# Three of four row tiles of the later quarters are transposed by DMA instead of TensorE, x is loaded a quarter ahead, one pool holds the PSUM banks, and VectorE adds into banks that are still accumulating

## The chip, the cores and the metric

The kernel runs on one core of one Trainium2 chip. The metric is the device time of one execution in microseconds (us), of which the median of several runs is taken. A profile shows one execution: its instructions on TensorE (PE for the products, PEld for loading their stationary operand), VectorE (DVE), ScalarE (ACT), GpSimd (POOL) and SyncE (SP), which only issues DMAs here, and the transfers of the DMA engines. "Span" is the time from the first to the last instruction of that execution.

## The reference

```python
def _A_ref(x, mem0, Wq, Wk, Wv, Wo, seg_len):      # S = 2048 rows, Dm = 1024, H = 32 heads of 128
    ...
    mem = mem0                                     # 8 rows
    for s in range(n_seg):                         # 64 segments of 32 rows, one after the other
        xs = x[:, s * seg_len:(s + 1) * seg_len, :].copy()
        h = jnp.concatenate([mem, xs], axis=1)
        q = jnp.einsum('btd,dhe->bhte', h, Wq)     # k and v likewise
        scores = jnp.einsum('bhqe,bhke->bhqk', q, k) * scale
        p = _softmax(jnp.where(mask[None, None], scores, -1000000000.0), axis=-1)
        o = jnp.einsum('bhqk,bhke->bhqe', p, v)
        o = jnp.einsum('bhte,hed->btd', o, Wo)
        mem = o[:, :M, :].copy()
        outs.append(o[:, M:, :])
    return jnp.concatenate(outs, axis=1)

def _B_ref(x, w1, b1, w2, b2):                     # F = 3584
    h = _gelu(jnp.einsum('bsd,df->bsf', x, w1) + b1)
    return jnp.einsum('bsf,fd->bsd', h, w2) + b2

x = A_x
xn = _layernorm(x, axis=-1)
return x + _A_ref(xn, ...) + _B_ref(xn, ...)
```

## The kernel before, in words

The kernel has two stages, one after the other. **The dense stage** computes x + _B_ref(xn) for all 2048 rows and keeps it in DRAM (R_n) for the second stage. **The segment stage** then goes through the 64 segments; each needs the 8 memory rows of the one before, so their order is fixed. In the segment stage 47 weight units of 512 KB stay in SBUF and 17 are streamed in each segment through a ring of six slabs; two of these 17 are kept in PSUM banks (kept) and copied from there by VectorE, the other 15 come by DMA from copies in DRAM (the tiles Wc_K, Wc_Q, Wc_V, Wc_O).

The dense stage works in four quarters of 512 rows (loop over tg), each of four row tiles of 128 rows (t). A quarter has two products. The first product (first_product, L498) takes the normalized, transposed x (xnT, two slabs) and w1, in 28 blocks (fb) of 8 matmuls each; ScalarE adds the bias (L572) and takes the sigmoid (L560), and VectorE does the rest of the gelu (L561, L576 to L580) into the tiles gT. The second product (L619) takes gT and w2: for each row tile and each half of the columns (nb) 28 matmuls accumulate in one PSUM bank. VectorE then adds the bias b2 to the bank (L626) and the bank to x (L627), and the row goes to R_n (keep_R, L448). PSUM banks come from a pool, mps: six in turn named ps, and two named pT.

During the second product of a quarter the x of the next one is prepared. At its start SP issues the four loads of x (load_x, L345), in the first quarter also the 15 copies of streamed units to DRAM (copies, L247 and L249) and the five fetches of resident units (EARLY). VectorE takes the statistics (ln_stats, L385), ScalarE the root (L394). Each row tile is normalized (ln_apply, L404) ahead of its part of the second product, and after it TensorE transposes it in eight 128x128 blocks (turned, L413) into a bank pT, from where VectorE and ScalarE copy one half each into xnT (turned_out, L418). After the last tile SP writes xnT to DRAM for the segment stage (keep_xT, L431 and L441), and then writes the finished rows of R_n in another order to res_d and resL_d (turn_R, L485), in 56 DMAs for a quarter; for the third quarter POOL issues them.

The last quarter's second product is written apart (L640 to L689). put_mem (L321) first brings the 8 memory rows into the first segment's x (hr_home, L325). Then all eight banks accumulate side by side: for the first 20 of the 28 fc all row tiles in turn (L647), the slabs of w2 and gT being refilled with resident units as they fall free (freed). For row tile 3 the bias and x are brought into the bank by four matmuls (L667 and L669). The last eight fc (TAIL) are done row tile by row tile, with the additions of tiles 0 to 2 on VectorE (L677, L678) behind them and the copies of tile 3 on ScalarE and VectorE (L686 to L688) at the end. The pool mps is then closed and a new one, banks, is opened: three banks acc in turn, one named mixed, and four named kept.

In the segment stage (products L791 and L1049) a streamed unit's slab is refilled as soon as TensorE is done with it (unit_done, start_stream, L268 and L279), by SP in the order of ORDERS. The order of the instructions of every engine is that of the program text (tc.manual_schedule). DMAs that SP and ScalarE issue share eight semaphores in turn (DMAHW0 to DMAHW7 in the built program): a DMA waits until the one before it on its semaphore has landed.

## Time and profile before

| what | value |
|---|---|
| median of 3 runs (lowest, highest) | 1813.58 us (1809.34, 1815.01) |
| the profiled execution's own time | 1810.81 us |
| its span | 1809.0 us |
| granted TensorE clock, mean | 0.999 |
| TensorE busy, whole span | 1702.7 us (94%) |
| dense stage | to about 414 us of the span |
| segment stage | from 414.70 us, first matmul of L791 |
| bytes moved by DMA | 592.07 MB, mean 327 GB/s |

A row of a timeline has the start, the duration, the engine, the line of the kernel, the operation, output and input, and in brackets the engine's idle time ahead of it with what ended that time. A row of a table by stretches has, for each engine, the busy time and in parentheses the number of instructions, then the granted clock of TensorE (1.00 is full speed), the mean busy share of the 16 DMA engines (it can read a little over 1) and GB/s. A row of waits has who waited for whom, the sum in us, the number of times and the longest. Matmuls overlap in the records: each is drawn some 380 ns long where they start 216 ns apart, so distances between starts are read, not durations.

### The profile page before, as it was taken

To read this page: it belongs to the slowest core of one execution; us is meant where nothing else is said; L and a number is where in the kernel's file an instruction comes from. 1 tells how busy PE (TensorE), PEld (TensorE's weight loads), DVE (VectorE), ACT (ScalarE), POOL (GpSimd) and SP (SyncE) were. 2 spreads that over 40 slices of the span, in tenths; PEclk is the share of its full clock that TensorE was granted. 3 is DMA by queue.
4 is the path that set the end of the run, shared out by engine and by line. 5 is a ranking of instruction groups with operands and counts; after the bars stand their busy time and mean duration, and the time that the engine had idled before them with its cause. 6 is when DMAs were issued, how large, how long until landed. Compare 5 with 4: busy or idle time off the path is not lost.

```text
span 1809.0 us, 71476 instructions
## 1 busy us (share of the span) xinstructions
PE 1702.7 (94%) x31161; PEld 894.6 (49%) x31161; DVE 983.8 (54%) x2517; ACT 686.6 (38%) x1698; POOL 300.5 (17%) x586
## 2 busy tenths in 40 slices
PE   8999999997999999999999999999999999999998
PEld 4444444444445555555554555554545555555544
DVE  7657483805555555555555555555555555555544
ACT  6334260702333333333333334343433334334333
POOL 0000000411132111111111212111111211111111
PEclk9999999999999999999999999999999999999999
DMA  9931111769999999999999999999999999999998
GB/s 289 310 100 48 53 48 37 247 221 339 370 385 389 376 385 374 386 374 379 387 380 380 385 396 388 384 389 364 382 384 375 387 369 393 380 375 392 384 390 315
DMA packets 221310, 592.07 MB, mean 327 GB/s; under 512 B 46195, under 2 KB 76515, under 8 KB 220996
## 3 DMA queue, kind: packets, MB, share of 16 engines
q1 hardware_dynamic: 197584, 567.08, 83.7%
q0 software_dynamic: 16896, 16.85, 2.9%
q8 instruction: 244, 4.00, 0.9%
q10 hardware_dynamic: 6516, 3.57, 0.7%
q14 instruction: 70, 0.57, 0.1%
HBM read 573.43 MB, written 28.90 MB: 333 GB/s over the span
## 4 chain that ended last, share of the span: by engine, by line
PE 78%; DMA 11%; DVE 4%; ACT 4%; issue 3%; ACTq 0%; DVEq 0%; POOL 0%; POOLq 0%
PE acc L791 38%; PE acc L1049 12%; PE ps L498 11%; PE ps L619 8%; DMA u<-Wc_O 7%; DMA u<-Wc_V 3%; PE ps L647 2%; ACT mixed L960 2%; PE acc L1000 1%; PE mixed L908 1%; DVE kq L875 1%; DVE pd_main L973 1%; ACT kq L870 1%; PE pT L647 1%; PE mixed L914 1%
## 5 line engine op out<-in xcount | busy, mean ns | idle before, releaser
L791 PE MATMUL acc<-u,hr_home 128*32 128x512 bf16 x11520 | 760.2, 380 | 16.7 <-issue 7.3
L791 PEld LDWEIGHTS <-hr_home 128*32 128x32 bf16 x12288 | 351.0, 96 | 286.0 <-issue 39.1
L791 PE MATMUL acc<-u,hrL 128*32 128x512 bf16 x2880 | 256.4, 380 | 6.4 <-issue 3.8
L498 PE MATMUL ps<-u 128*128 128x512 bf16 (+1 forms) x920 | 194.4, 374 | 2.0 <-ACT u L418 2.0
L268 DVE TENSOR_SCALAR u<-kept 128x512 uint32<-128x512 uint32 x254 | 163.2, 684 | 57.9 <-PE acc L791 43.4
L843 ACT CAST d_oL<-acc 128x512 bf16<-128x512 f32 x143 | 82.0, 584 | 263.3 <-PE acc L791 254.8
L619 PE MATMUL ps<-u 128*128 128x512 bf16 x672 | 147.0, 379 | 0.0
L1049 PE MATMUL acc<-u,d_oL 128*32 128x512 bf16 x1944 | 132.7, 381 | 9.7 <-issue 6.0
L498 PEld LDWEIGHTS <-u 128*128 128x128 bf16 x920 | 89.8, 98 | 104.9 <-issue 2.4
L1049 PEld LDWEIGHTS <-kq 128*32 128x32 bf16 x3908 | 102.7, 96 | 76.5 <-ACT kq L1019 21.8
L973 DVE TENSOR_TENSOR pd_main<-kq,mixed 128x320 bf16<-128x320 bf16 x128 | 62.5, 488 | 133.1 <-ACT mixed L960 133.1
L875 DVE STREAM_TRANSPOSE kq<-kq 128x512 bf16<-128x512 bf16 x128 | 91.1, 711 | 73.5 <-ACT kq L870 71.1
L870 ACT CAST kq<-acc 128x512 bf16<-128x512 f32 (+2 forms) x192 | 85.3, 444 | 114.5 <-PE acc L791 84.8
L1049 PE MATMUL acc<-u,kq 128*32 128x256 bf16 (+1 forms) x2372 | 116.0, 313 | 13.6 <-DMA u<-Wc_O 11.4
L1240 POOL DMA_DIRECT2D out_dram<-hr_home x168 | 85.2, 514 | 221.5 <-DVE hr_home L1207 221.1
L847 ACT CAST kq<-acc 128x512 bf16<-128x512 f32 x128 | 75.1, 587 | 111.6 <-PE mixed L914 105.5
L791 PEld LDWEIGHTS <-hrL 128*32 128x32 bf16 x3072 | 88.1, 96 | 59.0 <-issue 6.0
L938 DVE TENSOR_TENSOR kq<-kq,mixed 128x96 bf16<-128x96 bf16 (+1 forms) x256 | 38.1, 190 | 125.5 <-ACT kq L928 68.6
L619 PEld LDWEIGHTS <-u 128*128 128x128 bf16 x672 | 65.3, 98 | 77.4 <-DVE g_u L580 0.4
L1049 PEld LDWEIGHTS <-d_oL 128*32 128x32 bf16 x2592 | 65.3, 96 | 66.1 <-issue 20.0
L572 ACT ACTIVATE g_xb<-ps,b1col 128x512 bf16<-128x512 f32 x112 | 76.8, 686 | 55.5 <-PE ps L498 54.7
L960 ACT ACTIVATE mixed<-mixed,small_consts 128x160 f32<-128x160 f32 x256 | 94.2, 368 | 8.4
(133 smaller groups left out, 2010.4 us busy)
## 6 DMA issues: line engine op xcount, KB each, us to landing
u<-Wc_K SPq DMA_DIRECT2D x256, 512.0 KB
u<-Wc_V SPq DMA_DIRECT2D x256, 512.0 KB
u<-Wc_O SPq DMA_DIRECT2D x256, 512.0 KB
u<-Wc_Q SPq DMA_DIRECT2D x192, 512.0 KB
u<-in_B_w_dram SPq DMA_DIRECT2D x28, 512.0 KB
u<-in_A_Wq_dram SPq DMA_DIRECT2D x13, 512.0 KB
u<-in_A_Wv_dram SPq DMA_DIRECT2D x12, 512.0 KB
u<-in_A_Wk_dram SPq DMA_DIRECT2D x9, 512.0 KB
```

Of the source, the lines that this page charges most:

```text
L268: nc.vector.tensor_single_scalar(out=out, in_=in_, scalar=0, op=ALU.bitwise_or)
L498: nc.tensor.matmul(ps[:, SEG * s0:SEG * s1].rearrange("p (s t) -> p s t", t=SEG), lhsT=w1_sb[fb // 2][:, kt, (fb % 2) * P:(fb % 2 + 1) * P ...
L572: nc.scalar.activation(out=xb[:, :], in_=ps[:, :], func=ACT.Identity, bias=b1col[:, fb:fb + 1], scale=1.0)
L619: nc.tensor.matmul(ps[:, :], lhsT=gts[fc // 4][:, fc % 4, t * P:(t + 1) * P], rhs=w2_sb[fc // 2][:, fc % 2, cs], start=(fc == 0), stop=(fc ...
L791: nc.tensor.matmul(o, lhsT=lhs[:, i, :], rhs=m, start=(i == seq[0]), stop=(i == seq[-1]), tile_position=(0, 32 * j),)
L843: cp(out=out, in_=ps.rearrange("p (h e) -> p h e", e=32))
L870: nc.scalar.copy(out=q_home[:, h0:h1, NL:40], in_=ps[:, 32 * h0:32 * h1].rearrange("p (h e) -> p h e", e=32))
L875: nc.vector.transpose(out=home, in_=home)
L960: nc.scalar.activation(out=mixed[:, 160 * b:160 * b + 160], in_=mixed[:, 0:160], func=ACT.Exp, scale=-1.0, bias=off[:, b:b + 1],)
L973: nc.vector.tensor_tensor(out=pdA.rearrange("p c b q -> p b c q"), in0=prA[:, None, :, :].to_broadcast([P, 2, 4, 40]), in1=dd, op=ALU.mult,)
L1049: nc.tensor.matmul(acc[r0:r0 + rows, 0:256 * len(blocks)], lhsT=lhsT, skip_group_check=True, rhs=o_columns(t, k, blocks), start=start, sto ...
L1240: loads.dma_start(out=out_flat[rows, 256 * j:256 * j + 256], in_=res[32 * j:32 * j + NX, :])
```

## The change

- For quarters 2 to 4, three of the four row tiles (1, 2 and 3) are no longer transposed by TensorE. send_x cuts a normalized tile into eight pieces of 32 rows by 512 columns, and ScalarE issues for each a transposing DMA from the tile to xnT. Tiles 1 and 2 are normalized and sent ahead of the second product, tile 3 after its first row tile; tile 0 is normalized ahead of the third row tile and still transposed by TensorE behind it.
- x is loaded a quarter ahead: tiles 4 to 7 at the start, behind the weights; the others at the end of a second product, when the slabs of the quarter's x are free. The copies of streamed units and the fetches EARLY go from the start of the first quarter's second product to its end, behind those loads.
- One pool holds the eight PSUM banks from start to end, as six in turn (ps) and two (pT); the segment stage takes over the same tiles by name.
- put_mem moves from the start of the last second product into the last first product, behind block 20 (MEM_AT).
- In the last second product VectorE adds b2 and x into each bank while it accumulates, at fc 4, 6, ... 18 for banks 0 to 7 in turn: the bank's matmul of that fc is left out then and done together with the next one. The four matmuls with b2 and x go, and so does the tail by row tiles. Row tile 0 runs two fc (AHEAD) ahead of the others, and the rows are copied out at the end (row_out).

The diff, cut to its core:

```diff
@@ -49,7 +49,10 @@
-TAIL = 8
+AHEAD = 2
+ADD_FIRST = 4
+ADD_STEP = 2
+MEM_AT = 20
...
@@ -329,7 +332,19 @@
-    with tc.tile_pool(name="ma", bufs=2) as ma, tc.tile_pool(name="mps", bufs=6, space=PSUM) as mps:
+    banks = ctx.enter_context(tc.tile_pool(name="banks", bufs=1, space=PSUM))
+    turns = {"ps": deque(range(6)), "pT": deque((6, 7))}
+    place_of = {}
+
+    def new_ps(way="ps"):
+        k = turns[way][0]
+        turns[way].rotate(-1)
+        shape, kind = ([P, 512], F32) if way == "ps" else ([P, KT, P], BF16)
+        ps = banks.tile(shape, kind, name=way, tag=f"bank{k}")
+        place_of[id(ps)] = k, ps
+        return ps
+
+    with tc.tile_pool(name="ma", bufs=2) as ma:
...
@@ -373,6 +388,7 @@
+        xtoks.update({tt: load_x(tt) for tt in range(4, 8)})
...
@@ -408,7 +424,7 @@
         def turned(xn):
-            pT = mps.tile([P, KT, P], BF16, name="pT", bufs=2)
+            pT = new_ps("pT")
             for kt in range(KT):
                 nc.tensor.transpose(pT[:, kt, :], xn[:, kt * P:(kt + 1) * P], ident)
             return pT
...
@@ -424,6 +440,15 @@
+        def send_x(t, xn, xnT):
+
+            for i in range(4):
+                for half in range(2):
+                    nc.scalar.dma_start_transpose(
+                        out=xnT[half][:, 4 * t + i, :, :],
+                        in_=xn[SEG * i:SEG * i + SEG, 512 * half:512 * half + 512],
+                    )
...
@@ -581,6 +603,9 @@
+                if last and fb == MEM_AT:
+                    put_mem(o_sb, nxt["hT"], new_ps(), wide=False)
+                    nc.sync.dma_start(out=d_oL[:, 0:DM], in_=Wo_v[:, h + 1, :])
...
@@ -592,29 +617,28 @@
             if not last:
                 xnT = new_xnT(tg + 1)
-                for t in range(4):
-                    xtoks[4 * tg + 4 + t] = load_x(4 * tg + 4 + t)
-                if tg == 0:
-                    for unit, c in copies.items():
-                        fetch(c, unit)
-                    fetch_resident(*EARLY)
                 for t in range(4):
                     ln_stats(4 * tg + 4 + t)
                 ln_sqrt(4 * tg + 4, 4 * tg + 8)
                 ln_rstd(4 * tg + 4, 4 * tg + 8)
+                for t in (1, 2):
+                    send_x(t, ln_apply(4 * tg + t + 4), xnT)
                 for t in range(4):
                     ttg = 4 * tg + t
-                    xn = ln_apply(ttg + 4)
+                    if t == 1:
+                        send_x(3, ln_apply(4 * tg + 7), xnT)
+                    if t == 2:
+                        xn = ln_apply(4 * tg + 4)
                     rsb = xtoks[ttg]
                     for nb in range(2):
                         cs = slice(nb * 512, (nb + 1) * 512)
-                        ps = mps.tile([P, 512], F32, name="ps")
+                        ps = new_ps()
...
@@ -625,9 +649,14 @@
                             )
                         nc.vector.tensor_tensor(out=ps[:, :], in0=ps[:, :], in1=b2bc[:, cs], op=ALU.add)
                         nc.vector.tensor_tensor(out=rsb[:, cs], in0=ps[:, :], in1=rsb[:, cs], op=ALU.add)
-                        if nb == 1:
-                            turn_x(ttg + 4, xn, xnT)
+                        if nb == 1 and t == 2:
+                            turn_x(4 * tg + 4, xn, xnT)
                     keep_R(ttg, rsb)
+                xtoks.update({tt: load_x(tt) for tt in range(4 * tg + 8, min(4 * tg + 12, NT))})
+                if tg == 0:
+                    for unit, c in copies.items():
+                        fetch(c, unit)
+                    fetch_resident(*EARLY)
                 keep_xT(tg + 1, xnT)
                 for t in range(4):
...
@@ -636,72 +665,63 @@
                 start_stream("xn2")
                 start_stream("xn3")
-                put_mem(o_sb, nxt["hT"], mps.tile([P, 512], F32, name="ps"), wide=False)
-                nc.sync.dma_start(out=d_oL[:, 0:DM], in_=Wo_v[:, h + 1, :])
-                pss = [mps.tile([P, 512], F32, name="ps") for _ in range(6)]
-                pss += [mps.tile([P, 512], F32, name="pT", bufs=2) for _ in range(2)]
-                halves_of = [slice(512 * nb, 512 * nb + 512) for nb in range(2)]
-                x = xtoks[4 * tg + 3]
-
-                def second_product(fc, t, nb, stop):
+                pss = [new_ps() for _ in range(6)]
+                pss += [banks.tile([P, 512], F32, name="ps", tag=f"bank{k}") for k in turns["pT"]]
+                seg_banks = [place_of[id(ps)][0] for ps in pss[:6]] + list(turns["pT"])
+                taken = [0] * FC
+
+                def second_product(fc, t, nb):
                     nc.tensor.matmul(
                         pss[2 * t + nb][:, :],
                         lhsT=gts[fc // 4][:, fc % 4, t * P:(t + 1) * P],
-                        rhs=w2_sb[fc // 2][:, fc % 2, halves_of[nb]],
+                        rhs=w2_sb[fc // 2][:, fc % 2, nb * 512:nb * 512 + 512],
                         start=(fc == 0),
-                        stop=stop,
+                        stop=(fc == FC - 1),
+                        skip_group_check=True,
                     )
-
-                def freed(fc):
-                    if fc % 2:
-                        fetch_resident(f"w2_{fc // 2}")
-                    if fc % 4 == 3:
-                        fetch_resident(f"gT{fc // 4}")
-
-                for fc in range(FC - TAIL):
+                    taken[fc] += 1
+                    if taken[fc] == 8:
+                        if fc % 2:
+                            fetch_resident(f"w2_{fc // 2}")
+                        if fc % 4 == 3:
+                            fetch_resident(f"gT{fc // 4}")
+
+                def row_out(t, engines):
+                    x = xtoks[4 * tg + t]
+                    for nb, cp in enumerate(engines):
+                        cp(out=x[:, 512 * nb:512 * nb + 512], in_=pss[2 * t + nb][:, :])
+                    keep_R(4 * tg + t, x)
+
+                add_at = {ADD_FIRST + ADD_STEP * n: n for n in range(8)}
+                for step in range(FC + AHEAD):
                     for t in range(4):
+                        fc = step if t == 0 else step - AHEAD
+                        if not 0 <= fc < FC:
+                            continue
                         for nb in range(2):
-                            second_product(fc, t, nb, False)
-                    freed(fc)
-                for nb, cs in enumerate(halves_of):
-                    nc.tensor.matmul(pss[6 + nb][:, :], lhsT=ones[0:1, :], rhs=b2row[0:1, cs], start=False, stop=False)
-                for nb, cs in enumerate(halves_of):
-                    nc.tensor.matmul(pss[6 + nb][:, :], lhsT=ident, rhs=x[:, cs], start=False, stop=False)
-                for t in range(3):
-                    for fc in range(FC - TAIL, FC):
-                        for nb in range(2):
-                            second_product(fc, t, nb, fc == FC - 1)
-                    r = xtoks[4 * tg + t]
-                    for nb, cs in enumerate(halves_of):
-                        ps = pss[2 * t + nb]
-                        nc.vector.tensor_tensor(out=ps[:, :], in0=ps[:, :], in1=b2bc[:, cs], op=ALU.add)
-                        nc.vector.tensor_tensor(out=r[:, cs], in0=ps[:, :], in1=r[:, cs], op=ALU.add)
-                    keep_R(4 * tg + t, r)
-                for nb in range(2):
-                    for fc in range(FC - TAIL, FC):
-                        second_product(fc, 3, nb, fc == FC - 1)
-                        if nb:
-                            freed(fc)
-                    if nb == 0:
-                        nc.scalar.copy(out=x[:, 0:512], in_=pss[6][:, :])
-                nc.vector.tensor_copy(out=x[:, 512:768], in_=pss[7][:, 0:256])
-                nc.scalar.copy(out=x[:, 768:1024], in_=pss[7][:, 256:512])
-                keep_R(4 * tg + 3, x)
-    with tc.tile_pool(name="late", bufs=1) as late, \
-            tc.tile_pool(name="banks", bufs=1, space=PSUM) as banks:
+                            n = 2 * t + nb
+    with tc.tile_pool(name="late", bufs=1) as late:
...
 
-        free_banks = deque(f"acc{k}" for k in range(3))
+        free_banks = deque(f"bank{k}" for k in seg_banks[:3])
...
-        mixed = banks.tile([P, 512], F32, name="mixed")
+        mixed = banks.tile([P, 512], F32, name="mixed", tag=f"bank{seg_banks[3]}")
...
-        kept = banks.tile([P, 4, 512], F32, name="kept")
 
-            copy_bits(kept[:, bank, :].bitcast(U32), w.bitcast(U32))
-            kept_in.setdefault(unit, []).append((c0, kept[:, bank, :]))
+            copy_bits(kept[bank].bitcast(U32), w.bitcast(U32))
+            kept_in.setdefault(unit, []).append((c0, kept[bank]))
```

20 lines of the change are left out of this document (16 added, 4 removed).

## Prediction

> **What bounds the kernel now.** I read the table of stretches first, then TensorE's timeline of the dense stage, its waits, and SP's timeline.
>
> ```profile
> 161.00:212.00 51.00, 50.73 (x259) 23.93 (x258) 21.90 (x44) 5.51 (x10) 1.26 (x3) 1.00 0.04 16
> ...
> 425.00:450.00 25.00, 17.43 (x388) 8.93 (x384) 10.42 (x26) 6.68 (x20) 0.00 (x0) 1.00 1.04 397
> 450.00:1809.00 1359.00, 1270.09 (x28622) 692.32 (x28614) 722.26 (x1869) 516.86 (x1413) 253.00 (x477) 1.00 1.00 380
> ```
>
> The columns are busy times of PE, PEld, DVE, ACT, POOL, then clock, DMA share and GB/s. In a dense second product (161 to 212) TensorE is busy 50.73 of 51 us at full clock, while ACT works 5.51 us and the DMA engines stand at 0.04: what TensorE doesn't have to do there, the stage doesn't take. In the segment stage the DMA engines are full (1.00) and TensorE is busy 1270.09 of 1359 us; this stage is a balance of the two, and its first 25 us (17.43 busy) are its worst.
>
> ```profile
> 161.43 12.25 PE L619 MATMUL ps<-u 128*128 128x512 bf16 x56
> 173.52 0.61 PE L413 MATMUL pT<-hr_home,ln_xn 128*128 128x128 bf16 x8
> 173.96 12.25 PE L619 MATMUL ps<-u 128*128 128x512 bf16 x56
> ...
> 211.12 0.61 PE L413 MATMUL pT<-hr_home,ln_xn 128*128 128x128 bf16 x8
> 212.40 48.51 PE L498 MATMUL ps<-u 128*128 128x512 bf16 x224 [0.67 <-ACT u L418]
> ```
>
> A row tile of the second product takes 173.52-161.43 = 12.09 us (56 matmuls, 0.2158 each), its transposes 173.96-173.52 = 0.44 us. The fourth ends at 211.12+0.44 = 211.56, and the next product starts at 212.40, 0.84 us later, behind ScalarE's copy. A quarter's second product is thus 48.34 + 4x0.44 + 0.84 = 50.94 us.
>
> ```profile
> 360.15 0.23 PE L321 MATMUL ps<-ident_mem,d_oL 128*32 128x32 bf16 x8
> 360.31 1.25 PE L647 MATMUL ps<-u 128*128 128x512 bf16 x5
> 363.60 0.38 PE L647 MATMUL ps<-u 128*128 128x512 bf16 x1 [2.03 <-DVE hr_home L325]
> ...
> 398.83 0.60 PE L667 MATMUL pT<-b2row,ones 1*128 1x512 bf16 x2
> ...
> 399.80 10.52 PE L647 MATMUL ps<-u 128*128 128x512 bf16 x48
> 410.16 3.62 PE L647 MATMUL pT<-u 128*128 128x512 bf16 x16
> 414.70 0.61 PE L791 MATMUL acc<-low,hr_home 128*32 128x512 bf16 x8 [0.92 <-ACT u L688]
> ```
>
> ```profile
> 362.00:364.00 2.00, 0.41 (x2) 0.19 (x2) 1.12 (x4) 0.63 (x1) 0.76 (x2) 1.00 0.87 211
> 364.00:366.00 2.00, 2.00 (x7) 0.75 (x6) 0.00 (x0) 0.00 (x0) 0.00 (x0) 0.63 0.80 215
> 366.00:368.00 2.00, 2.00 (x6) 0.76 (x5) 0.00 (x0) 0.00 (x0) 1.05 (x2) 0.52 0.94 375
> ```
>
> The last second product: 160 matmuls from 360.31 to 398.83 take 38.52 us where 160x0.2158 = 34.53 would do. 2.03 us of the excess of 3.99 is the wait for the memory rows, the rest (1.9) the clock of 0.63 and 0.52 right behind that wait; the span's mean clock of 0.999 leaves 1.8 us for the whole of it, so there is no second such place. The four matmuls for b2 and x take 399.80-398.83 = 0.97 us, and from the last matmul's end (410.16+16x0.2158 = 413.61) to the first segment are 1.09 us.
>
> **The change, part by part**, against the profiled execution (1810.81 us, 1.81 beyond its span, 2.77 under the median of the three runs).
>
> *TensorE's share.* Nine of the twelve transposed tiles of quarters 2 to 4 go: 9x0.44 = 4.0 us. The gap of 0.84 us ahead of each next product goes too, if xnT is complete: TensorE's one tile is turned behind the third row tile, 12 us early. 3x0.84 = 2.5 us. In the last quarter the wait for the memory rows (2.0) goes, as put_mem stands eight blocks earlier, where the clock's dip goes with it (1.9); the four matmuls go (0.9, as the same columns of bank matmuls remain); and row tile 0 ends two fc early, so that its two banks are copied while 18 matmuls (3.9 us) still run: the 1.09 us become about 0.1, so 1.0. Sum: 4.0+2.5+3.9+0.9+1.0 = 12.3 us.
>
> The dip could also have another cause than the wait ahead of it and stay; that is part of rival 3. The Trainium skill, TensorE: Matmul & The Clock Gate, "Part 1: The HAM clock gate", speaks for this: there the clock is halved only after an idle window of about 3.4 us. By that rule the sum is 1.9 us less; the trace, with a dip right behind 2.03 us of idle, does not agree with it.
>
> *What ScalarE and DMA take on.* Each quarter gets 24 transposing DMAs, and the trace has none.
>
> ```profile
> L448 ACTq DMA_DIRECT2D R_n<-u x4: 326/342/359, 406.0 to 414.7; - x4
> L485 SPq DMA_DIRECT2D res_d<-R_n x66: 537/610/1492, 119.5 to 251.9; - x66
> L431 SPq DMA_DIRECT2D rows_d<-u x8: 385/1314/7793, 44.4 to 313.0; - x8
> hr_home<-rows_d POOLq DMA_DIRECT2D x56, 64.0 KB, 5.7
> 164.66 1.28 DVE L385 BATCH_NORM_STATS2 ln_stats<-u 128x6 f32<-128x512 bf16 x2
> 170.40 0.30 ACT L394 ACTIVATE ln_rstd<-ln_mv,eps_t 128x4 f32<-128x4 f32 x1 [4.81 <-DVE ln_mv L387]
> 170.94 0.55 DVE L404 TENSOR_SCALAR ln_xn<-u,ln_mv,ln_rstd 128x1024 bf16<-128x1024 bf16 x1
> 211.76 0.58 ACT L418 COPY u<-pT 128x512 bf16<-128x512 bf16 x1 [10.60 <-PE pT L413]
> ```
>
> Issuing one costs ScalarE from 0.34 us (whole rows, the median of L448) to 1.31 us (the most finely cut transfer, 256-byte pieces, the median of L431). These 32 KB are nearest to res_d's small pieces: I take 0.61. The time that there is: statistics, root and first ln_apply are done at 170.94+0.55, 10 us into the second product; the next product starts 48.34+0.44 = 48.8 us in. So 38.8 us for 24, or 1.6 us each. At 0.61 they take 15 us, at 1.31 31 us. ScalarE has nothing else there but half a copy (0.58 us), so the cost is nothing in either case; the cover is these 38.8 us, and beyond 1.6 us each tenth of a microsecond costs 2.4 us in each of three quarters. The data: with eight semaphores, eight can be in flight; if each landed only after the 5.7 us of a 64 KB load, three rounds are 17 us, hidden too. The one price for the operation itself is in the Trainium skill, VectorE: DVE Perf Modes, "The three transpose paths": 1309 ns for a 128x128 block by DMA, as many elements as a piece here, against 390 ns on TensorE, which it advises. By it an estimate for 24 is 31 us, hidden, and the sum is the same; no run here shows it.
>
> What waits behind them: tile 3's ln_apply reuses tile 1's buffer and stands in VectorE's queue until its eight DMAs have landed, and the additions that free banks stand behind it; TensorE has four other banks, 6 us each, so 24 us of cover. Tile 0's ln_apply needs tile 2's DMAs landed by 36 us into the product, as TensorE stops there otherwise: 10+16x0.61+5.7 = 25 us; at 1.31, 37 us, a stop of about 1 us.
>
> *SP's queue.* The 15 copies and five fetches move from the start to the end of the first quarter's second product.
>
> ```profile
> 58.46 2.94 SPq L247 DMA_DIRECT2D Wc_O<-in_A_Wo_dram  x4
> 83.08 2.24 SPq L249 DMA_DIRECT2D u<-in_A_Wk_dram  x2
> 98.00:104.00 6.00, 6.00 (x35) 2.97 (x34) 2.17 (x4) 0.58 (x1) 0.48 (x1) 1.00 0.12 44
> 119.52 1.33 SPq L485 DMA_DIRECT2D res_d<-R_n  x2
> 154.65 0.61 SPq L485 DMA_DIRECT2D resL_d<-R_n  x1
> ```
>
> SP needed 58.46 to 85.3 to issue them, the transfers ran until about 98, and the 56 DMAs of turn_R took 119.52 to 155.3, 0.64 each. After: last row kept at about 112, x and copies from 115, done 36 to 40 us later (about 153), turn_R's 32nd DMA at 153+20 = 173, landed by 178. In the built order the second quarter's first transposing DMAs wait on the shared semaphores for turn_R's 23rd to 32nd, so they begin up to 9 us later than 10 us in, of 38.8. Hidden at 0.61 (10+9+15+5.7, 40 of 48.8 us), 7 us late at 1.31 in this quarter alone. The moved loads of x stand ahead of the copies and are not late.
>
> *VectorE, and the end of the stage.*
>
> ```profile
> 403.24 0.70 DVE L677 TENSOR_TENSOR ps<-ps,b2bc 128x512 f32<-128x512 f32 x1 [39.70 <-PE ps L647]
> ```
>
> ```profile
> 413.39 0.59 ACT L686 CAST u<-pT 128x512 bf16<-128x512 f32 x1 [50.44 <-PE pT L647]
> ...
> 415.03 1.28 ACT L698 ACT_TABLE_LOAD   x1 [0.39 <-ACT u L688]
> 417.52 0.58 ACT L843 CAST d_oL<-acc 128x512 bf16<-128x512 f32 x1 [1.20 <-PE acc L791]
> ```
>
> There are 16 additions of 0.70 us, four more than before, two for a bank. A bank is left alone from one fc to the second after it, some 15 matmuls or 3.2 us for 1.4 us of additions: nothing; the cover is 1.8 us. ScalarE gets four copies (0.59), three issues (0.34) and the table load (1.28) around the last matmul, from 0.7 us ahead of it: it is free for the first key copy 4.0 us behind it, where that copy came 417.52-414.70 = 2.8 us behind the first product before. Up to 1.2 us late, beside queries that TensorE does meanwhile; I take 0, since the stall that follows absorbs it.
>
> *The start of the segments.*
>
> ```profile
> 413.42 2.97 SPq L247 DMA_DIRECT2D u<-in_A_Wo_dram  x4
> 402.00:414.00 12.00, 11.78 (x55) 5.22 (x54) 8.25 (x13) 0.59 (x1) 3.83 (x7) 1.00 0.34 103
> ```
>
> ```profile
> PE acc L791 <- DMA u<-Wc_Q: 2.8, 2, 1.7
> PE acc L791 <- DMA u<-Wc_V: 1.8, 4, 0.9
> ```
>
> Six slabs fell free only in the last 1.7 us before (four issues of L247 at 413.42 among them), 3 MB, while the DMA engines stood at 0.34 in the 12 us ahead. Now four of the six go at the products' pace, one fc per 1.7 us: 2 MB less ahead of Wc_Q, or 5 us at the 397 GB/s of 425 to 450. The waits for Wc_Q in the first two segments are 2.8 us. I take 3; bounds 0 (another wait takes its place) and 5. Nothing else in the segment stage changes: its streams keep order and distances.
>
> **Sum.** 12.3+3 = 15.3 us: 1810.81-15.3 = 1795.5 for an execution like the profiled one, and 1813.58-15.3 = **1798 us** for the median. With the bounds (dense 10.4, if the dip stays, to 13, start 0 to 5, and the spread of the three runs around their median, -4.2 to +1.4) the forecast's own range is 1791 to 1805.
>
> **Rivals.**
>
> 1. *The transposing DMAs run late* (the side of slower). For it: no row shows one, they cut the data into columns of 32 elements where the finest transfer of the trace has rows of 256 bytes, and tile 3's stand behind two landings. Against: ACT and DMA are all but idle in the 51 us of that product. It decides at 1.6 us apiece for the first loss and at 1.6+15.3/72 = 1.8 us for break-even. At 2.5 us each: 72x0.9 = 65 us lost, 1798+65 = 1863.
> 2. *They just miss*: 1.3 to 1.8 us apiece, or the second quarter's semaphores: 2 to 15 us lost, 1800 to 1813, I say 1807.
> 3. *The clock's dip stays*, and a wait of the segments' start takes Wc_Q's place: 1798+1.9+2.8 = 1803. For it the full DMA engines of 425 to 450 (1.04); against it, that the dip follows its wait at once. The rule of the Trainium skill on the clock, above, speaks for its first part.
> 4. *The start gains more*: with 2 MB ahead, the shares of Wc_V and Wc_O in the first two segments go too, and DMA, full throughout, keeps the lead to the end: 1798-6 = 1792, inside the range.
>
> ```profile
> PE acc L1049 <- DMA u<-Wc_O: 13.5, 27, 1.4
> ```
>
> Against it: in 450 to 1809 TensorE waits only 13.5 us for Wc_O, so a lead of DMA is worth little there.
>
> **How the numbers follow.** The forecast 0.50, rival 1 0.17, rival 2 0.15, rival 3 0.10, rival 4 0.08. About 0.3% (5.4 us) is what a measurement of this kernel can tell from no change, so faster means under 1808.1: the forecast, rivals 3 and 4, and three fifths of rival 2 are 0.77; I leave 0.03 of it to the middle case, as rival 2's edge lies close: 0.74. Within 0.3%: that 0.03, the rest of rival 2 and 0.01 of rival 1, 0.10. Slower: 0.16. The range reaches from rival 4 and the runs' spread (1788) over rival 2 (1813, with spread 1816); it leaves out rival 1 and 0.02 below, 0.18.
>
> **What would show it.** Right: in the second products of the later quarters one row of eight L434 transposes instead of four, and the next product's first matmul 0.2 us behind the last; 24 DMA issues of ACT per quarter within 35 us of the start; no wait at the first L674 matmuls and a clock of 1.00 from 360 on; the first segment's product 0.1 us behind the last L674; Wc_Q's waits gone. Wrong: TensorE waiting for ACT's queue or DMA at the third row tile's end or at a quarter's start (rivals 1 and 2), a dip of the clock in the last quarter without a wait (3), or a segment stage longer than the 1394 us from 414.70 to the end.

## The result and the profile after

1798.61 us median (1795.51 to 1799.76, six runs) against 1814.01 for the kernel before, six runs on the same chip: the ratio is 0.9924, its 95% interval 0.9902 to 0.9945, so 15.4 us less where 15.3 were forecast. The profiled execution took 1797.63 us, its span 1795.9.

TensorE's timeline of the dense stage, after (start, length, line, tiles, count; rows left out are marked; a few matmul records are missing, as in x164 for 168):

```profile
63.05 36.43 PE L643 MATMUL ps<-u 128*128 128x512 bf16 x164
99.32 0.61 PE L429 MATMUL pT<-hr_home,ln_xn 128*128 128x128 bf16 x8
99.77 12.25 PE L643 MATMUL ps<-u 128*128 128x512 bf16 x55
111.86 48.51 PE L523 MATMUL ps<-u 128*128 128x512 bf16 x224
...
160.20 36.42 PE L643 MATMUL ps<-u 128*128 128x512 bf16 x164
197.51 0.62 PE L429 MATMUL pT<-hr_home,ln_xn 128*128 128x128 bf16 x8 [0.88 <-DVE ln_xn L420]
197.96 12.25 PE L643 MATMUL ps<-u 128*128 128x512 bf16 x55
210.05 48.51 PE L523 MATMUL ps<-u 128*128 128x512 bf16 x224
258.40 36.42 PE L643 MATMUL ps<-u 128*128 128x512 bf16 x164
...
307.19 36.42 PE L523 MATMUL ps<-u 128*128 128x512 bf16 x168
...
355.80 48.51 PE L674 MATMUL ps<-u 128*128 128x512 bf16 x219
404.24 0.61 PE L811 MATMUL acc<-low,hr_home 128*32 128x512 bf16 x8
```

One row of transposes a quarter is left, the next product follows the last row tile at once (99.77+12.09 = 111.86), and the last product runs its 224 matmuls in 48.44 us without a hole. One wait is new: 0.88 us in the second quarter. The second products take 48.81, 49.85 and 48.79 us (the third from 258.40 to 307.19), where they took 50.98, 50.97 and 50.97.

What ScalarE does in the same time: its timeline, and the durations of line 448 (min/median/max in ns).

```profile
72.52 32.10 ACTq L448 DMA_TRANSPOSE u<-ln_xn  x24
...
174.00 32.76 ACTq L448 DMA_TRANSPOSE u<-ln_xn  x24
...
268.53 31.78 ACTq L448 DMA_TRANSPOSE u<-ln_xn  x24
```

```profile
L448 ACTq DMA_TRANSPOSE u<-ln_xn x72: 1178/1257/2203, 72.5 to 299.1; - x72
```

A transposing DMA occupies ScalarE's queue for 1.257 us (the median), twice the 0.61 that the forecast took; 24 of them fill 32 of the 38.8 us that hide them.

TensorE's longest waits at the start of the segments (400 to 450; who waited for whom, sum in us, times, longest), and the first and last memory rows of the segment stage (line 318 after, line 315 before; the two times are the first and the last start):

```profile
PE acc L811 <- DVE qL L863: 2.0, 2, 1.8
PE acc L1069 <- DMA u<-Wc_O: 1.6, 2, 0.9
PE acc L811 <- DMA u<-Wc_V: 0.4, 1, 0.4
```

```profile
L318 PE MATMUL mixed<-ident_mem,kq x158: 169/176/190, 439.7 to 1770.5; 128*128 128x32 bf16 x94, 128*128 128x16 bf16 x64
```

```profile
L315 PE MATMUL mixed<-ident_mem,kq x158: 169/177/191, 452.4 to 1783.4; 128*128 128x32 bf16 x94, 128*128 128x16 bf16 x64
```

The waits for Wc_Q (2.8 us before) are gone. From the first segment matmul to the first memory rows it was 452.4-414.70 = 37.7 us, and is 439.7-404.24 = 35.5; from there to the last ones it was 1331.0 and is 1330.8.

The two spans, then, differ by 13.1 us: the three second products give 5.5, the last quarter from the end of the third one 5.9 (102.99 before, 97.05 after), the segments 2.6 (1394.3 before, 1391.7 after, 2.2 of it before the first memory rows); the first 16 us took 0.9 more (the granted clock was 0.89 there, 1.00 before: it dipped to half from 11.8 to 15.2 us; the last section shows when it does).

### The profile page after: what moved, and what is told of

It is laid out like the page before. It is cut to its first block, busy times and chain, and to the rows that moved or that the text cites. A ratio compares the mean times of both kernels' runs of the same rounds, so it can differ in the third digit from the quotient of the medians.

```text
span 1795.9 us, 71439 instructions
## 1 busy us (share of the span) xinstructions
PE 1701.3 (95%) x31065; PEld 892.2 (50%) x31085; DVE 984.2 (55%) x2514; ACT 683.8 (38%) x1692; POOL 300.4 (17%) x586
## 4 chain that ended last, share of the span: by engine, by line
PE 76%; DMA 12%; DVE 4%; ACT 4%; issue 3%; ACTq 1%; POOL 0%; DVEq 0%; POOLq 0%; SPq 0%
PE acc L811 38%; PE acc L1069 13%; PE ps L523 11%; DMA u<-Wc_O 7%; PE ps L643 7%; DMA u<-Wc_V 4%; PE ps L674 3%; ACT mixed L980 1%; PE acc L1020 1%; PE mixed L928 1%; DVE kq L895 1%; ACTq L448 1%; DVE pd_main L993 1%; DMA u<-Wc_K 1%; ACT kq L890 1%
## 5 line engine op out<-in xcount | busy, mean ns | idle before, releaser
L1069 PE MATMUL acc<-u,kq 128*32 128x256 bf16 (+1 forms) x2372 | 119.9, 319 | 14.4 <-DMA u<-Wc_O 12.2
```

The costliest lines, as they stand in the source:

```text
L1069: nc.tensor.matmul(acc[r0:r0 + rows, 0:256 * len(blocks)], lhsT=lhsT, skip_group_check=True, rhs=o_columns(t, k, blocks), start=start, sto ...
```

## The experiments

For every kernel the trace is cut in three: *dense* from the long first product's first matmul (16.63 in the changed kernel) to the first segment matmul, *start* from there to the first memory rows of a segment, *middle* from there to the last ones. The kernels e1 to e4, then e0, e5, e6, e8, then the rest ran on one chip each with the kernel before, whose medians there were 1809.21, 1811.61 and 1810.56.

| kernel | dense | start | middle | median | ratio to before, interval |
|---|---|---|---|---|---|
| before | 399.0 | 37.7 | 1331.0 | 1814.01 | 1 |
| changed | 387.6 | 35.5 | 1330.8 | 1798.61 | 0.9924 (0.9902 to 0.9945) |
| e0 changed again | 388.0 | 35.7 | 1328.0 | 1797.91 | 0.993 (0.9904 to 0.9955) |
| e1 all by TensorE | 393.1 | 36.0 | 1333.5 | 1803.74 | 0.9957 (0.9931 to 0.9982) |
| e2 TensorE, early | 390.6 | 35.2 | 1329.1 | 1798.49 | 0.9941 (0.9915 to 0.9966) |
| e3 copies first | 390.5 | 36.1 | 1324.1 | 1793.53 | 0.9907 (0.9878 to 0.9936) |
| e4 memory rows late | 389.5 | 35.6 | 1322.9 | 1795.79 | 0.9921 (0.9893 to 0.9948) |
| e5 late fetches | 393.7 | 36.9 | 1326.2 | 1793.65 | 0.9904 (0.9873 to 0.9935) |
| e6 four by DMA | 414.9 | 36.4 | 1329.8 | 1824.76 | 1.0077 (1.0049 to 1.0105) |
| e7 half size | 467.7 | 35.6 | 1335.8 | 1879.24 | 1.0371 (1.0332 to 1.0409) |
| e8 two queues | 430.7 | 36.4 | 1324.2 | 1840.20 | 1.0173 (1.0138 to 1.0208) |
| e9 copies split | 386.6 | 36.2 | 1334.4 | 1795.02 | 0.9917 (0.9885 to 0.9949) |
| e10 old tail | 387.3 | 39.7 | 1324.1 | 1799.80 | 0.994 (0.9917 to 0.9963) |
| e11 memory rows alone | 395.1 | 37.9 | 1327.1 | 1808.03 | 0.9994 (0.9977 to 1.001) |

The three come from one profile of each kernel. The middle holds the same work in all of them and lies anywhere from 1322.9 to 1335.8. Executions of one kernel spread no less (the 23 of the kernel before on the last chip took 1802.96 to 1821.32), so the medians hide differences of 2 or 3 us. The dense stage repeats to some tenths where its waits do (387.6 and 388.0), so steps of that size are read from it, not from the medians.

### e0: the changed kernel again

> The changed kernel once more, as the measure for the three kernels beside it on the same chip. Both theories: 1798.6 as far as this chip is like the first one; its dense stage ends within 1 us of 404.2, and the first row of memory rows for a segment (the ident_mem matmuls of the segment stage) stands 35.5 us behind the first segment matmul, where it stood 37.7 us behind it before the change.

1797.91, ratio 0.993; dense 388.0, start 35.7. The second quarter's wait was 1.31 us this time.

### e1 and e2: the turning back on TensorE

In e1 all `send_x` calls go and each tile is turned behind its own row tile:

```
-                for t in (1, 2):
-                    send_x(t, ln_apply(4 * tg + t + 4), xnT)
...
+                    xn = ln_apply(ttg + 4)
...
-                        if nb == 1 and t == 2:
-                            turn_x(4 * tg + 4, xn, xnT)
+                        if nb == 1:
+                            turn_x(ttg + 4, xn, xnT)
```

> The changed kernel with all four tiles of a quarter turned by TensorE, each behind its own row tile as before the change; everything else as changed. Theory (the nine tiles' transposes and the three gaps at the quarters' ends are what the DMAs save, and one wait of 0.88 us in the second quarter is what they cost): 4.0 + 2.5 - 0.9 = 5.6 us more than the changed kernel's 1798.6, so 1804.2; in the trace four rows of eight transposes per quarter and three second products of 50.9 us. Rival (the dense gain comes from the banks and the loads of x, not from the transposes): 1798.6.

In e2 the fourth tile is turned with the third, behind the third row tile: `for k, xn in zip(((0,), (1,), (2, 3), ())[t], xns): turn_x(...)`.

> As e1, but the fourth tile is turned behind the third row tile, with the third, so that the next product's input is ready 12 us early. Theory: the gaps of 0.84 us go without any DMA; left over are nine transposes of 0.44 us, and the second quarter's wait of 0.88 us is gone: 1798.6 + 4.0 - 0.9 = 1801.7, second products of 50.1 us. Rival (the gap needs the DMAs, as the copies out of the banks come late): 1804.2.

The end of the first quarter in TensorE's timeline, e1 and then e2:

```profile
112.71 0.61 PE L429 MATMUL pT<-hr_home,ln_xn 128*128 128x128 bf16 x8
113.99 48.51 PE L523 MATMUL ps<-u 128*128 128x512 bf16 x224 [0.67 <-ACT u L434]
```

```profile
99.54 1.06 PE L429 MATMUL pT<-hr_home,ln_xn 128*128 128x128 bf16 x16
100.43 12.25 PE L638 MATMUL ps<-u 128*128 128x512 bf16 x54
112.52 48.51 PE L523 MATMUL ps<-u 128*128 128x512 bf16 x224
```

With the fourth tile turned last the gap is back (0.67 us idle behind ScalarE's copy); turned one row tile earlier it is gone without any DMA. Dense: e1 393.1-387.6 = 5.5 us more than the changed kernel (5.6 expected), e2 3.0 more (3.1). So the DMAs themselves bring 3 of the 15 us. The medians agree with that and can't show it alone: e2's interval overlaps that of the changed kernel.

### e3 and e9: where SP's copies stand

e3 puts the block `if tg == 0: for unit, c in copies.items(): fetch(c, unit) ... fetch_resident(*EARLY)` back ahead of the statistics of the first quarter's second product.

> The changed kernel with the 15 copies and the five early fetches issued at the start of the first quarter's second product, as before the change. Theory (the second quarter's wait of 0.88 us comes from SP's transfers of R being late, by shared semaphores): that wait goes, and the transposing DMAs of the first quarter, 1.26 us each, still end before 111 us although the DMA engines are full: 1798.6 - 0.9 = 1797.7. Rival (a transposing DMA queues behind 10 MB of copies, which run until about 98 us): the first eight land at about 98, sixteen more of 1.26 us end at 118 to 120, where the first product of the next quarter should have begun at 111.9: 7 to 9 us lost, 1806 to 1808.

TensorE's and ScalarE's timelines in that product, and the stretch behind the wait (its last columns are clock, DMA share, GB/s):

```profile
100.44 0.62 PE L429 MATMUL pT<-hr_home,ln_xn 128*128 128x128 bf16 x8 [2.03 <-DVE ln_xn L420]
100.89 13.94 PE L647 MATMUL ps<-u 128*128 128x512 bf16 x55
114.67 48.51 PE L523 MATMUL ps<-u 128*128 128x512 bf16 x224
```

```profile
71.44 37.99 ACTq L448 DMA_TRANSPOSE u<-ln_xn  x24
```

```profile
102.00:104.00 2.00, 2.00 (x6) 0.76 (x5) 1.34 (x3) 0.00 (x0) 0.50 (x3) 0.50 0.90 265
```

Both were partly right. The second quarter's wait is gone (its second product, from 163.01 to 211.81, takes 48.80 us). In the first the 24 issues take 38 us instead of 32, though the median of one stays at 1.258: 4 of the 6 us are gaps between two, the longest from 78.13 to 81.13, where ScalarE waits for a semaphore that it shares with a copy (which lands at 81.11). It is not the next product that waits, as the rival had it, but tile 0's ln_apply, which needs tile 2's buffer: 2.03 us, and then the clock falls to 0.50 and costs 1.7 more. Dense is 2.8 us longer. The best median of all, 1793.53, comes with a middle of 1324.1 and says nothing for this placing.

e9 splits the copies and gives the second quarter's transfers of R to GpSimd:

```
-                if tg == 0:
-                    for unit, c in copies.items():
+                if tg < 2:
+                    for unit, c in list(copies.items())[5 * tg:5 + 99 * tg]:
                         fetch(c, unit)
+                if tg == 1:
                     fetch_resident(*EARLY)
...
-                    turn_R(4 * tg + t, nc.gpsimd if tg == 2 else nc.sync)
+                    turn_R(4 * tg + t, nc.gpsimd if tg else nc.sync)
```

> The changed kernel with ten of the 15 copies and the five early fetches a quarter later, and the second quarter's transfers of R issued by GpSimd, so that SP has issued the first quarter's transfers of R before the second quarter's transposing DMAs begin. Theory (the wait in the second quarter, 0.88 us in the first profile of the changed kernel, 1.31 in the second, 4.72 and a dip in the kernel e5, comes from shared semaphores with transfers that SP issues late): all three second products take 48.8 us, the dense stage ends 0.9 to 1.3 us earlier, and 1 to 2 us go on average, 1797. Rival (ScalarE's transposing DMAs in that quarter wait for something else): the second quarter keeps its wait, no difference. Second rival (the copies of the second quarter's end make the third quarter's transposes late): the wait moves to the third quarter.

SP's timeline of the second quarter in the changed kernel, with ScalarE's DMAs from 174.00 on, and e9's ScalarE and TensorE there:

```profile
173.38 1.20 SPq L510 DMA_DIRECT2D res_d<-R_n  x2
...
177.38 4.57 SPq L510 DMA_DIRECT2D res_d<-R_n  x2
184.75 0.61 SPq L510 DMA_DIRECT2D resL_d<-R_n  x1
```

```profile
170.15 32.24 ACTq L448 DMA_TRANSPOSE u<-ln_xn  x24
```

```profile
160.03 36.42 PE L643 MATMUL ps<-u 128*128 128x512 bf16 x164
196.29 0.61 PE L429 MATMUL pT<-hr_home,ln_xn 128*128 128x128 bf16 x8
196.73 12.25 PE L643 MATMUL ps<-u 128*128 128x512 bf16 x55
208.82 48.51 PE L523 MATMUL ps<-u 128*128 128x512 bf16 x224
```

In the changed kernel SP's transfers of R and ScalarE's transposes hold each other up: ScalarE begins at 174.00, 13.8 us into the product (9.5 in the first quarter), and from 177 on SP's pace falls too. The semaphore events of the trace show the link: ScalarE's first transposing DMA waits for a shared semaphore that SP's transfer issued at 172.03 completes on landing, at 173.91 (in e5 the landing comes at 175.91, and ScalarE begins at 176.01). With e9's transfers issued by 167.4, ScalarE begins 10.1 us in, right behind its ln_apply, and TensorE waits for nothing. All three second products take 48.8 us, and the dense stage is the shortest of all, 386.6, 1.0 and 1.5 less than in the two executions of the changed kernel. It is the version to keep, for that trace; its median, 1795.02, and its ratio can't be told from the changed kernel's.

### e4 and e11: the memory rows

e4 moves the two lines of `put_mem` and the load of d_oL from the first product's block 20 to behind `start_stream("xn3")`, where they were; e11 does the opposite, alone, on the kernel before.

> The changed kernel with the memory rows put in their bank between the last quarter's two products, as before the change, not eight blocks earlier. Theory (the dip of TensorE's clock follows the wait): wait of 2.0 and dip of 1.9 come back, 1798.6 + 3.9 = 1802.5, clock under 0.7 for about 4 us behind the wait. Rival (the dip had another cause): only the wait, 1800.6, and no dip. Second rival (the stage that follows absorbs it, being bound by DMA): 1798.6.

> The kernel before, with nothing changed but the memory rows put in their bank eight blocks earlier. Theory (the dip of the clock follows the wait of 2.03 us): wait and dip go, the dense stage ends at 410.8 instead of 414.7, 3.9 us less than before, 1810. Rival (the dip has another cause): 2.0 us less, 412.7, and a clock under 0.7 near 362 us. Second rival (what is gained is given back at the segments' start, which waits for its streams): 410.8, but the first ident_mem matmul comes no earlier than before, at 452.4.

TensorE's timelines (e4's start of the last product; e11's first segment matmul), and a stretch of e11:

```profile
355.90 2.12 PE L673 MATMUL ps<-u 128*128 128x512 bf16 x8
359.15 46.56 PE L673 MATMUL ps<-u 128*128 128x512 bf16 x211 [1.13 <-DVE hr_home L328]
```

```profile
411.72 0.61 PE L792 MATMUL acc<-low,hr_home 128*32 128x512 bf16 x8 [0.92 <-ACT u L689]
```

```profile
364.00:366.00 2.00, 2.00 (x11) 0.91 (x10) 0.42 (x1) 0.08 (x1) 1.02 (x2) 1.00 0.77 268
```

e11 bears the theory out: from the end of the first product (361.22) to the segments it is 50.50 us, where it was 54.55 from 360.15, so 4.05 less, with the clock at 1.00; the whole dense stage is 3.9 shorter, as forecast, since 0.16 us of it only moved ahead. Its gain is not given back at the start either (37.9 against 37.7). Its median, 2.5 us under the one before, has an interval that holds 0 and 4: the whole says nothing. e4 shows where the theory reached too far: the wait is 1.13 us, no dip follows, and dense is 1.8 more (1.3 of it here, from 307.31 to 405.64, the rest the second quarter's wait of 1.43), not 3.9. In the changed order row tile 0 runs two blocks ahead, so eight matmuls stand before the bank that waits, where five did. So the new order alone takes 0.9 of the 2.03 us off the wait, as far as e4 shows, and what is left is too short for a dip: in the changed kernel the move of the memory rows is worth 1.3 us, not 3.9.

### e5 and e10: how the segments start

e5 issues the last six fetches only when the last of the 28 blocks (fc) has been taken:

```
-                    if taken[fc] == 8:
+                    if taken[fc] == 8 and (fc < FC - 8 or fc == FC - 1):
```

> The changed kernel with the last six slabs of the dense stage fetched for the segments only when the last product has taken its last block, as before the change, instead of at the products' pace. Theory (2 MB less ahead of the segments' first streams is worth 2 to 3 us): the dense stage ends as in the changed kernel, the first ident_mem matmul stands 37 to 38 us behind the first segment matmul instead of 35.5, with waits for Wc_Q of about 2.8 us, and the time is 2 to 3 us over the changed kernel's. Rival (the shorter start came from somewhere else, such as the freer ScalarE at the end): 35.5 and no difference.

Nothing was tested by it: a fetch waits for the last matmul that reads its slab, wherever the program has it, and that matmul hadn't moved. SP had issued its last slab of Wv before 404.72 and four of Wo by 411.2, as far behind the product's pace as in the changed kernel. What its trace shows is the second quarter's wait at its worst, in code that is still that of the changed kernel:

```profile
201.28 1.03 PE L429 MATMUL pT<-hr_home,ln_xn 128*128 128x128 bf16 x8 [4.72 <-DVE ln_xn L420]
202.10 14.12 PE L643 MATMUL ps<-u 128*128 128x512 bf16 x56
```

4.72 us, and 2.2 us more for the clock (transposes 0.82 instead of 0.45, row tile 13.95 instead of 12.09).

e10 moves the matmuls themselves: up to block 20 as before, then eight blocks of each row tile in turn, the copies behind each.

```
-                for step in range(FC + AHEAD):
+                for step in range(FC - 8):
...
+                    for fc in range(FC - 8, FC):
+                        for nb in range(2):
+                            second_product(fc, t, nb)
+                    row_out(t, engines)
```

> The changed kernel with the end of the last product as before the change: the last eight blocks row tile by row tile, so that six slabs fall free only in the last 1.7 us and the last bank's copy is waited for; the additions into banks stay on VectorE, the four matmuls for b2 and x stay out. (In e5 the release of the slabs followed the last matmul that reads each, whatever the place of the fetch in the program, so it kept the early release.) Theory (the early release is what makes the segments' start shorter, and the copy's wait what ended the stage): 1.0 us for the gap at the end of the stage, Wc_Q waits of about 2.8 us in the first two segments, the first ident_mem matmul 37.7 us behind the first segment matmul instead of 35.6: together 3 us over the changed kernel, 1801. Rival (the start is shorter for another reason): the gap alone, 35.6, 1799.

TensorE's timeline at the end of e10's last product, ScalarE's last copy of a bank, and TensorE's waits for Wc_Q from 403 to 444:

```profile
355.30 48.51 PE L674 MATMUL ps<-u 128*128 128x512 bf16 x219
403.74 0.61 PE L821 MATMUL acc<-low,hr_home 128*32 128x512 bf16 x8
```

```profile
404.31 0.37 ACT L724 CAST u<-ps 128x256 bf16<-128x256 f32 x1 [1.60 <-DVE u L723]
```

```profile
PE acc L821 <- DMA u<-Wc_Q: 3.0, 2, 1.9
```

The Wc_Q waits are back, 3.0 us, and the start is 39.7. Of all 14 traces these waits appear in three, before (2.8), e10 (3.0) and e11 (2.3), the three that free the slabs late, with starts of 37.7 to 39.7; in the other eleven the start is 35.2 to 36.9. That settles the start: the early release is worth 1 to 4 us. But the gap of 1.09 us at the end did *not* come back (355.30 to 403.74 is 48.44, as in the changed kernel). Before, the first segment matmul waited for ScalarE's last copy (0.92 us, line 688); in e10 that copy begins 0.57 us behind the first segment matmul, which no longer waits for it. What lets it go ahead is the one pool of banks: it can take the bank of a row tile copied long ago, where a pool of its own had to wait for the last copy. Of the medians, 1799.8 against 1797.91 goes the expected way, within their spread.

### e6, e7 and e8: the price of a transposing DMA

e6 sends the fourth tile by DMA too (`send_x(0, ln_apply(4 * tg + 4), xnT)` at t == 2, no `turn_x`).

> The changed kernel with all four tiles of a quarter turned by DMA, 32 issues of ScalarE per quarter instead of 24. Theory (ScalarE's issue of 1.26 us each is what bounds them, and 24 fill 32 of 38.8 us of cover): the 32 end about 42 us behind the first, which is 115 in the first quarter against 111.4 for the next product, so 5, 10 and 6 us are lost in the three quarters and 1.9 us for a dip of the clock behind each, less 1.3 for the three tiles that TensorE doesn't turn: 1798.6 + 25 = 1824. Rival (the issues overlap and only their landing counts, the cover is ample): 1798.6 - 1.3 = 1797.3.

e7 cuts each DMA in two: `for q in range(2): nc.scalar.dma_start_transpose(out=xnT[half][:, 4 * t + i, 2 * q:2 * q + 2, :], in_=...256 columns)`.

> The changed kernel with each transposing DMA cut in two, 32 rows by 256 columns instead of 32 by 512: 48 issues per quarter, the same bytes. Theory (ScalarE's 1.26 us is a price per DMA): 48 take 60 us, 30 more than 24, of which 5 to 7 us are covered in the first and third quarter and 4 in the second, so some 75 us more, 1875. Rival (the 1.26 us is a price per element, of writing out the transfer's pieces): 0.63 us each, 30 us per quarter, 1798 as the changed kernel. Between the two, a fixed part and a part per element: each tenth of a microsecond per issue over 0.75 costs 4.8 us in each of three quarters.

TensorE's and ScalarE's timelines of e6, then e7's durations and the first quarter of its ScalarE:

```profile
115.54 1.86 PE L523 MATMUL ps<-u 128*128 128x512 bf16 x4 [3.97 <-DMA u<-ln_xn]
...
230.62 49.98 PE L523 MATMUL ps<-u 128*128 128x512 bf16 x224 [13.26 <-DMA u<-ln_xn]
...
333.07 37.87 PE L523 MATMUL ps<-u 128*128 128x512 bf16 x168 [4.12 <-DMA u<-ln_xn]
```

```profile
72.51 42.62 ACTq L448 DMA_TRANSPOSE u<-ln_xn  x32
```

```profile
L449 ACTq DMA_TRANSPOSE u<-ln_xn x144: 1169/1250/2240, 72.7 to 382.0; - x144
```

```profile
72.66 62.87 ACTq L449 DMA_TRANSPOSE u<-ln_xn  x48
```

1824.76 for e6 against 1824 expected: 32 issues need 42.6 us, and the next products wait 4.0, 13.3 and 4.1 us (and 1.0 more in the first). The total agrees better than its parts: the second wait is 3 us longer than expected. 1879.24 for e7 against 1875: half the bytes take 1.250 us where all took 1.257. Between these two sizes it is a price per DMA, paid in ScalarE's queue (both have 32 rows; fewer rows were not tried), and the cover of 38.8 us is real: with 24 it just holds, with 32 it doesn't.

e8 sends two tiles from ScalarE and two from SP, with e9's moves (`send_x(..., nc.scalar if t == 1 else nc.sync)`, tile 3 by ScalarE, tile 0 by SP).

> All four tiles of a quarter turned by DMA, two begun by ScalarE and two by SP, 16 issues each; to leave SP free for them, ten of the fifteen copies and the five early fetches stand a quarter later, and GpSimd issues the transfers of R of the second quarter too. Theory (the issue on one queue is the bound, so two queues halve it): the 32 are issued in about 22 us, no wait in the second quarter, no transposes of TensorE in the second products of 48.4 us: 1.3 + 0.9 us less than the changed kernel, 1796.4. Rival (the transposing DMAs share one thing behind the queues and take 1.26 us each whichever queue begins them): 40 us for 32, as in e6, and 1805 to 1824.

The theory fell, and 1840.2 lies beyond the rival's range too. The durations of line 448, ScalarE's between 80 and 92 us and SP's of the whole run:

```profile
L448 ACTq DMA_TRANSPOSE u<-ln_xn x3: 1177/1177/1177, 82.1 to 91.4; - x3
```

```profile
L448 SPq DMA_TRANSPOSE u<-ln_xn x48: 1161/1237/2077, 79.6 to 346.5; - x48
```

The two queues take turns: ScalarE's start at 82.06, 86.75 and 91.37, SP's at 84.42 and 89.04, one each 2.33 us, so an alternation costs 1.1 us beyond the 1.2 of a DMA. SP's first waits until 79.6 for those of ScalarE, and its second eight, behind two rows that it keeps for the residual, until 113.1 for ScalarE's second eight. So the 32 take from 71.84 to 123.74 in the first quarter, 51.9 us, where one queue took 42.6. The Trainium skill, DMA: Bandwidth & Descriptors, "Silent corruption: two transposing streams in flight at once", demands that the later stream wait for the earlier one's completion; the built program has such waits, and the trace agrees with them: no two overlap (ScalarE's at 82.06 waits for the semaphore of SP's of 79.62). Whether transposing DMAs would run faster side by side was not tried.

## Why the prediction was right, point by point

- **Transposes and gaps** (4.0+2.5): 5.5 in the profiles, as the second quarter gave back 1.0 (a wait of 0.88). e1 and e2 split the sum as forecast, 3.0 for the transposes less the wait, 2.5 for the gaps. That the gaps need no DMA was in the forecast's reason (the last tile is turned 12 us early) and is shown by e2.
- **The issue of a transposing DMA**, taken as 0.61, is the mis-sized term: 1.257 us. It lies inside the bounds (0.34 to 1.31; of the three rows behind them only the 0.34 is ScalarE's), and the cover of 1.6 apiece held, so the sum didn't change; e6 shows how near the edge it was, 32 issues already lose 26 us. The figure that the forecast quoted from the Trainium skill (1309 ns for a 128x128 block, VectorE: DVE Perf Modes, "The three transpose paths") was the nearer one here, though e7 shows that half a block costs the same. The landing was mis-sized the other way: tile 3's ln_apply ran at 84.05, 11.5 us behind the first of the eight issues that it waits for, so about 1 us behind the last, not 5.7.
- **Rival 2** came true in its place and at about a tenth of its price: the second quarter's transposes begin 4.3 us later than the first's, and tile 0's ln_apply is late as the forecast said it would be at 1.31 us. 0.6 to 1.4 us, once 4.7 with a dip; e9 removes it. **Rival 1** needs more than 1.6 us per issue in every quarter; e6 and e7 are what it looks like.
- **Memory rows and the dip** (2.0+1.9): 4.05 in e11. The dip follows its wait; rival 3's first part is out. That is the price in the kernel before. In the changed kernel e4 gives the move 1.3; the other 2.6 already go with the new order of row tiles, which the forecast priced at nothing here.
- **Four matmuls** (0.9) and **the end gap** (1.0): both gone, as 48.44 us shows. The reason given for the gap, that row tile 0 ends early and is copied meanwhile, is only half of it: in the kernel before it ended early too, 48 matmuls ahead of the end, and the gap was there. e10 has that old order with the common pool and no gap, so the pool is the part that was missing. Whether the two blocks ahead are needed with it was not run.
- **The start** (3): 2.2 to the first memory rows, with the Wc_Q waits gone as forecast. Another wait takes part of their place in some executions: that for the rows of the left-over tokens (hrL) is 0.8 us before, absent in the changed kernel's profile, 1.6 in e0 and 1.8 in e6. Rival 4 is not seen.
- **The sum.** The profiles differ by 13.1 us and the medians by 15.4; the 2.3 between lie within the spread of executions, and no trace shows an effect behind them. That 15.4 meets the forecast's 15.3 so closely is luck. In the profiles, on which the sum was built, the parts are 5.5 of 6.5 (transposes and gaps), 5.9 of 5.8 (last quarter) and 2.6 of 3 (segments), less 0.9 for a dip of the clock in the first 16 us, which is chance: e0, the same kernel, has none there.

## What to carry to other kernels

Moving work off the bounding engine was worth 3 us here, and doing the same work one step earlier 2.5: try the order first. Before work goes to another queue, multiply its price per instruction by their number and hold it against the time that hides it; here 24 fitted and 32 didn't. And where the whole moves by a few tenths of a per cent between executions, a step of a microsecond is read from the stage in which it lies.

## What the runs showed of the hardware

- ScalarE's transposing DMA costs its queue 1.257 us for 32 KB and 1.250 for 16 KB, SP's 1.237 (medians, all of 32 rows).
- In e3, where copies filled the DMA engines for the first 12 us (share 1.02 from 72 to 84), the same 24 took 38.0 us instead of 32.1; the median of one was 1.258.
- A dip of TensorE's clock followed every single wait of 2.03 us or more in the dense stage (2.03 before and in e3, 3.97 and 4.12 in e6, 4.72 in e5, 13.3 in e6) and none of 0.55, 0.88, 1.13, 1.31 or 1.43 us. It cost 1.3 to 2.9 us, and 4.0 in the first quarter of e6, where a wait of 1.01 us came behind the first; longer waits did not cost more than short ones.
- What decides is a grid of time. In the traces' records of the granted clock every dip is a stretch of 3.41 us at 0.5, or several in a row, and all those of one execution begin on one grid of that step: in e6 at 11.77, 114.17, 219.98 and 332.62 us, 30, 31 and 33 steps apart. With each grid laid over TensorE's rows, the 14 traces hold 7322 steps at full clock. All 33 in which TensorE was busy less than 42% of the step were followed by a dip, and none of the 7245 in which it was busy more than 52%; between, 11 of 44 were (the busy shares are rough, as the ends of matmuls are modelled). The two waits of 2.03 us each lay within one step (40 and 41% busy); by the same shares an estimate for such a wait cut in half by the grid, 70% busy in both steps, is no dip, so the 1.9 us behind it are not a fixed price. The Trainium skill, TensorE: Matmul & The Clock Gate, "Part 1: The HAM clock gate", has a window of 3413 ns that runs freely, and the clock halved after an idle one. The length and the free running agree with the traces; that a window must be idle throughout does not.
- In the segment stage, 30 to 41 us behind its start, seven of the 14 traces show such a dip (3.41 us, twice that in e10) with no wait of 2 us ahead of it, and seven none, among them both kinds of the same kernel (the changed one and e0). The grid tells them apart in the main: the step ahead of the seven dips was 41 to 52% busy, the least busy one there in the other seven 49 to 61%. In the changed kernel it lay at 431.61, 45% busy; e0's least busy one was 53% busy. The two stretches of the changed kernel (last columns are clock, DMA share, GB/s; the first number behind the length is TensorE's busy time):

```profile
431.61:435.03 3.42, 1.54 (x32) 0.68 (x25) 2.19 (x6) 0.49 (x2) 0.00 (x0) 1.00 1.04 404
435.03:438.44 3.41, 3.34 (x60) 2.46 (x59) 1.33 (x3) 0.74 (x2) 0.00 (x0) 0.50 1.04 399
```
